# Local and pooled attention ahead of two MoE layers on one core: exponentials of two batches moved to ScalarE, a fixed table of constant products, new urgencies

## The chip, the core and the metric

The kernel runs on one core of a Trainium2 chip. The time is that of the whole program on the device, in microseconds (us); less is better. The engines named below are TensorE (PE; its weight loads PEld), VectorE (DVE), ScalarE (ACT), GpSimd (POOL) and SyncE (SP), which here only issues DMAs.

## The reference

Input q, k, v: 4 batches, 8 heads, 576 positions, 64 columns. Attention is the sum of two parts. The pooled part averages q, k and v over groups of 4 positions (144 left), does a full softmax attention on them and repeats each row 4 times. The local part is softmax attention within 3 positions to either side.

```python
q_d = q.reshape(B, H, Sd, factor, D).mean(axis=3)   # k_d, v_d alike
out_up = np.repeat(sm_attn(q_d, k_d, v_d), factor, axis=2)
scores = np.where(np.abs(i - j) < factor, scale * q @ k.T, -1e9)
out = out_up + softmax(scores) @ v
x = out.transpose(0, 2, 1, 3).reshape(2304, 512)
x = ((x @ w_a) * (x @ w_b)) @ w_out              # first MoE, d_ff 1536
h = x @ w_in
out = (max(h, 0) + alpha * min(h, 0)) @ w_out2   # second MoE, d_ff 2048
```

The four MoE weight matrices come in as float64 (read as int64 words).

## The kernel before

**Plan.** The kernel does not issue instructions directly. Every call goes to a `Plan` (line 22) that records the operation, the regions it reads and writes, and an estimated duration (`cost`, line 94; DMAs in `__call__`, line 128). When all is recorded, `reschedule` (line 214) builds each engine's order by list scheduling: among the ready operations of an engine the one with the highest priority goes first, and a priority is the estimated length of the work behind the operation plus a bias. The bias comes from the call and from the table `URGENT` (line 292) by the name of the operation's group, which `group` (line 1301) derives. Consecutive matmuls inside `with pe()` form one operation; the MoE's groups are chained in a fixed order (`pe(True)`). `fill` (line 257) then looks for planned gaps on TensorE and puts products of a constant bf16 tile (128x128 by 128x256) into them, as many as a share of the gap holds, into a bank that the next group overwrites. `issue` (line 282) sends everything out. Each engine then runs its own list in order and waits on semaphores.

**Attention.** A batch is 6 window tiles of 96 queries and 104 keys, all 8 heads at once. For one tile: `load` (line 670) brings k, q and v by three DMAs; `turn` (678) transposes q and k on TensorE, copies them from PSUM on ScalarE, and VectorE sums groups of four positions for the pooled part; `bound` (693) takes the largest absolute v on VectorE; `soft` (707) adds the mask and the scores into two PSUM banks of four heads, then for each bank VectorE takes the maximum of each row and subtracts it, ScalarE does one exponential over all 832 elements, and VectorE sums, inverts and scales; `p_turn` (731) transposes the probabilities; `av_t` (740) multiplies by v; `x_add` (756) adds the pooled part and splits the sum into two float16 halves in `xt`. The pooled part of a batch: `g_top`, `g_minus`, `g_exp`, `g_out` and `od_turn` for batches 0 and 1; `g_soft`, `g_turn` and `g_av` for 2 and 3. `batch_scale` (786) turns the bounds of a batch into a power of two by `pow2_abs` (440); `pow2_ss` (448) does the same from a sum of squares. Of the eight PSUM banks three ("a") serve attention, four ("m") the MoEs (two of these also the first turns, "h"), one ("r") small maxima.

**MoE.** Matrices are multiplied as three float16 products of high and low halves. `wab_chunk` (993) prepares one of six chunks of w_a and w_b: VectorE narrows float64 words to float32 (three operations of 128x1024 per matrix, `narrow`, line 508), ScalarE squares them for a bound, and ScalarE and VectorE split them (`split`, line 457). `s1` (925) does the first MoE's first products for half a batch: two sums of 12 matmuls of 288 columns, a ScalarE copy out of PSUM, three further operations. `s2`, `s3` and `s4` are the later products; the chain interleaves halves of batches so that attention of the later batches fits beside.

**Order of the recording.** `seq` (from line 1117) lists the head: constants, loads, then turns, softmaxes and the pooled attention of batch 0 interleaved tile by tile, for tiles 0 to 2; tiles 3 to 5, the weight chunks, batches 1 to 3 and the MoEs follow by nominal times.

The lines that the change touches are the DMA estimate (150), `fill`, `URGENT`, `bank` (397), `setup1`, `turn`, `bound`, `soft`, `av_t`, `od_turn`, `x_add`, `batch_scale`, the order of `seq`, `group` and the call of `fill` at the end.

## Time and profile before

| | us |
|---|---|
| median of 3 runs | 1003.62 (1002.61 to 1004.06) |
| the profiled execution, its own time | 1003.87 |
| its span, first to last instruction | 1002.1 |
| TensorE busy | 977.7 (98%) |
| TensorE weight loads busy | 672.5 (67%) |
| VectorE busy | 608.3 (61%) |
| ScalarE busy | 434.4 (43%) |
| GpSimd busy | 39.5 (4%) |

A busy time is the sum over an engine's instructions of that execution, as a share of the span. Constant products count as busy TensorE. All instructions carry line 285, where the plan issues them, so groups are told apart by the tiles that they write and read: `zone` is the large scratch area (attention tiles, later the second MoE's weights), `nm` and `nz` the softmax's maxima and sums, `vst` the bounds on v, `wab` and `wo` the first MoE's weights, `xt` its input, `tm` and `gt` its intermediate tiles, `m`, `a` and `r` the PSUM banks.

### The profile page before, as it was taken

To read this page: it belongs to the slowest core of one execution; us is meant where nothing else is said; L and a number is where in the kernel's file an instruction comes from. 1 tells how busy PE (TensorE), PEld (TensorE's weight loads), DVE (VectorE), ACT (ScalarE), POOL (GpSimd) and SP (SyncE) were. 2 spreads that over 40 slices of the span, in tenths; PEclk is the share of its full clock that TensorE was granted. 3 is DMA by queue.
4 is the path that set the end of the run, shared out by engine and by line. 5 is a ranking of instruction groups with operands and counts; after the bars stand their busy time and mean duration, and the time that the engine had idled before them with its cause. 6 is when DMAs were issued, how large, how long until landed. Compare 5 with 4: busy or idle time off the path is not lost.

```text
span 1002.1 us, 18185 instructions
## 1 busy us (share of the span) xinstructions
PE 977.7 (98%) x7488; PEld 672.5 (67%) x7488; DVE 608.3 (61%) x1293; ACT 434.4 (43%) x919; POOL 39.5 (4%) x81
## 2 busy tenths in 40 slices
PE   6988999999999999999999999999999999999998
PEld 4666777778877788777877777645546455464553
DVE  6899999876657566678987585612406135061340
ACT  3335566544424343335435364623516235162350
POOL 3001300012000200000000000000000000000000
PEclk9999999999999999999999999999999999999999
DMA  9596451144201512323343401010100100200000
GB/s 204 159 270 173 108 153 42 26 75 86 50 1 25 111 26 58 102 67 109 111 159 129 130 1 48 1 43 22 32 32 1 43 22 9 78 2 11 22 1 31
DMA packets 95938, 69.45 MB, mean 69 GB/s; under 512 B 71152, under 2 KB 78704, under 8 KB 95856
## 3 DMA queue, kind: packets, MB, share of 16 engines
q1 hardware_dynamic: 95856, 68.31, 25.2%
q8 instruction: 58, 0.95, 0.4%
q14 instruction: 24, 0.20, 0.1%
HBM read 58.86 MB, written 9.44 MB: 68 GB/s over the span
## 4 chain that ended last, share of the span: by engine, by line
PE 84%; DVE 13%; issue 1%; ACT 1%; DMA 0%; POOL 0%; DVEq 0%; POOLq 0%
PE m L285 75%; PE a L285 8%; DVE wab L285 4%; DVE zone L285 3%; DVE wo L285 2%; DVE nz L285 1%; DVE gt L285 1%; PE r L285 1%; DVE nm L285 1%; DVE tm L285 0%; DVE xt L285 0%; DMA zone<-in_v_dram 0%; DVE vst L285 0%; ACT wo L285 0%; ACT wab L285 0%
## 5 line engine op out<-in xcount | busy, mean ns | idle before, releaser
L285 PEld LDWEIGHTS <-wab 128*128 128x128 f16 x3168 | 306.4, 98 | 161.0 <-issue 4.2
L285 PE MATMUL m<-xt,wab 128*128 128x288 f16 x2304 | 296.2, 286 | 2.5 <-DVE xt L285 2.1
L285 PE MATMUL m<-xt,zone 128*128 128x384 f16 x1152 | 188.2, 326 | 0.0
L285 PE MATMUL m<-zone,wab 128*128 128x512 f16 x864 | 187.7, 379 | 0.0
L285 PEld LDWEIGHTS <-zone 128*128 128x128 f16 x1152 | 112.7, 98 | 74.9
L285 DVE SCALAR_TENSOR_TENSOR gt<-tm,nal,tm 128x384 f32<-128x384 f32 x96 | 59.3, 618 | 160.8 <-ACT tm L285 149.2
L285 PEld LDWEIGHTS <-wo 128*128 128x128 f16 x1152 | 111.8, 98 | 29.5 <-issue 0.8
L285 ACT ACTIVATE tm<-m 128x384 f32<-128x384 f32 (+1 forms) x224 | 95.3, 468 | 65.6 <-PE m L285 65.6
L285 PE MATMUL m<-gt,wo 128*128 128x288 f16 x864 | 110.3, 288 | 0.0
L285 DVE SCALAR_TENSOR_TENSOR wab<-gt,kap,wab 128x384 f16<-128x384 f32 x96 | 59.3, 618 | 58.2 <-ACT wab L285 58.2
L285 ACT ACTIVATE wab<-gt,kap 128x384 f16<-128x384 f32 x96 | 59.0, 615 | 58.1 <-DVE gt L285 58.1
L285 ACT ACTIVATE gt<-m,uf 128x512 f32<-128x512 f32 x18 | 12.4, 687 | 154.2 <-PE m L285 154.2
L285 ACT COPY zone<-a 104x384 f32<-104x384 f32 (+4 forms) x124 | 53.1, 471 | 53.1 <-PE a L285 52.8
L285 PE MATMUL a<-zone 64*96 64x104 f32 (+4 forms) x1104 | 72.8, 265 | 0.6 <-DVE zone L285 0.5
L285 PEld LDWEIGHTS a<-zone 64*96 64x96 f32 (+4 forms) x1104 | 58.4, 149 | 19.9 <-issue 14.6
L285 ACT ACTIVATE zone<-zone 96x832 f32<-96x832 f32 (+3 forms) x49 | 41.9, 855 | 51.8 <-DVE zone L285 49.0
L285 ACT COPY tm<-m 128x288 f32<-128x288 f32 x96 | 37.8, 394 | 43.1 <-PE m L285 40.7
L285 DVE SCALAR_TENSOR_TENSOR tm<-m,tm 128x288 f32<-128x288 f32 x96 | 43.0, 448 | 21.3 <-PE m L285 18.1
L285 ACT ACTIVATE gt<-tm 128x288 f16<-128x288 f32 x72 | 31.6, 440 | 44.4 <-DVE tm L285 44.3
L285 PE MATMUL a<-idf,zone 96*104 96x96 f32 (+4 forms) x392 | 41.6, 247 | 3.8 <-DVE sx L285 1.9
L285 POOL TENSOR_TENSOR zone<-zone 72x256 f32<-72x256 f32 x36 | 31.7, 893 | 307.9 <-DMA zone<-in_v_dram 167.2
L285 DVE SCALAR_TENSOR_TENSOR zone<-zone 128x512 int32<-128x512 int32 (+3 forms) x48 | 40.8, 861 | 0.4
(173 smaller groups left out, 810.5 us busy)
## 6 DMA issues: line engine op xcount, KB each, us to landing
zone<-in_moe_w_in_dram SPq DMA_DIRECT2D x8, 1024.0 KB
zone<-in_moe_w_out_dram SPq DMA_DIRECT2D x16, 512.0 KB
wo<-in_moe_w_a_dram SPq DMA_DIRECT2D x6, 1024.0 KB
wo<-in_moe_w_b_dram SPq DMA_DIRECT2D x6, 1024.0 KB
x_d<-x2s SPq DMA_DIRECT2D x8, 576.0 KB
out_dram<-gt SPq DMA_DIRECT2D x18, 256.0 KB
zone<-in_k_dram SPq DMA_DIRECT2D x21, 208.0 KB
zone<-in_v_dram SPq DMA_DIRECT2D x21, 208.0 KB
```

Of the source, the lines that this page charges most:

```text
L285: f(*args, **kw)
```

## The change

- `soft`: for batches 0 and 1 (`EXPH`) VectorE still takes the maxima, multiplies them by -scale, and ScalarE does one exponential per head (96x104) straight from PSUM, with the maximum as bias and the row's sum as a second output. The two subtractions and the separate sum on VectorE go for these batches.
- `bound`: for batches 0 and 1 (`NORM`) ScalarE squares v and sums it in place of VectorE's maximum; the squares go into the tile's `xt_z` buffer, where nothing reads them. `batch_scale` takes `pow2_ss` for them.
- The tuples `POOLP` and `JOIN` are empty: pooled sums stay on VectorE and `x_add` stays as it is. `setup4` builds a table `up_m` on GpSimd that only the `JOIN` branch reads.
- `fill` takes a table `FILLS`: so many constant products (bf16 tile `warm`, 128x128 by 128x256) go ahead of the named TensorE groups, counted in the order of recording, into the upper half of bank r. There are 187 in 28 places, each issued whatever the plan's gaps are.
- Names that begin with soft, pturn or av of tiles 0 to 2, and the pooled attention of batch 0, take PSUM banks from five (three "a", two "m").
- In the head all six turns come first, then the pooled attention with the softmaxes between, and `p_turn` and `av_t` of tiles 0 to 2 last. Loads are recorded in two calls (k and q; v) with names of their own.
- The planner's estimate of a DMA's rate and issue, the groups' names and the whole table `URGENT` are new.

The diff, with the two tables of urgencies and the branches of empty tuples cut:

```diff
--- before.py
+++ after.py
@@ -147,9 +147,9 @@
             for c in parts:
                 nb *= c
             run = min(min(int(x.ap[-1][1]) for x in (kw["out"], kw["in_"])) * SIZE[el.dtype], 4096)
-            rate = 230e3 if run >= 1024 else 150e3
+            rate = 300e3 if run >= 2048 else 220e3 if run >= 1024 else 195e3
             o.dma = (nb / rate, 2.2)
-            o.dur += 1.0
+            o.dur += 0.8
         else:
             d, o.lag = self.cost(eng, method, out, ins, kw)
             o.dur += d
@@ -254,30 +254,14 @@
         self.order = order
         return order
 
-    def fill(self, t0, t1, chain, early, stat, mov, each):
-
-
...
+    def fill(self, counts, out, stat, mov):
+
+
+        groups = [o for o in self.ops if o.eng == self.PE]
+        for k, n in counts.items():
+            if k < len(groups):
+                o = groups[k]
+                o.calls = [(self.nc.tensor.matmul, (out, stat, mov), dict(start=True, stop=True))] * n + o.calls
 
     def issue(self):
         for o in self.order:
@@ -285,36 +269,47 @@
                 f(*args, **kw)
 
 
-WAY = (0,0,0,0,0)
-
-
-URGENT = {"": -180, "alphas": -80, "bs0": -40, "bs1": 120, "bs2": 35, "bs3": 140, "gexp0": -20, "gexp1": -130,
...
+WAY = (0, 0, 0, 0, 0)
+EXPH, POOLP, NORM, JOIN = (0, 1), (), (0, 1), ()
+NUP = 1
+EARLY = [f"{k}{n}" for k in ("soft", "pturn", "av") for n in range(3)] + ["gtop0", "gminus0", "gexp0", "gout0", "odt0"]
+
+
+FILLS = {0: 22, 2: 3, 9: 4, 11: 4, 17: 1, 18: 1, 19: 3, 20: 2, 28: 5, 29: 5, 30: 4, 31: 11, 35: 1, 37: 2, 38: 6,
+          41: 1, 50: 28, 53: 13, 55: 8, 56: 2, 60: 39, 65: 6, 71: 1, 82: 7, 86: 1, 90: 3, 160: 3, 176: 1}
+
+
+URGENT = {"alphas": -10, "b0@0": 10, "b0@1": 110, "b0@2": 25, "b0@3": -75, "b0@4": -30, "b0@5": 35, "b@1": -80,
...
 
 LAST = None
 
@@ -392,9 +387,12 @@
              "a": [psum.tile([128, 512], F32, name=f"a{i}") for i in range(3)],
              "r": [psum.tile([128, 512], F32, name="r0")]}
     banks["h"] = banks["m"][:2]
+    banks["x"] = banks["a"] + banks["m"][:2]
     nbank = dict.fromkeys(banks, 0)
 
     def bank(tag):
+        if tag == "a" and P.name in EARLY:
+            tag = "x"
         nbank[tag] += 1
         return banks[tag][(nbank[tag] - 1) % len(banks[tag])]
 
@@ -460,6 +458,7 @@
 
     idf = const.tile([128, 128], F32, name="idf")
     ones = const.tile([2, 128], F32, name="ones")
+    warm = const.tile([128, 256], BF16, name="warm")
     floor = const.tile([128, 1], F32, name="floor")
 
     def top_of(m, n):
@@ -608,6 +607,7 @@
     xt_z = [t.rearrange("p (a n) -> p a n", a=KD) for t in
             [const.tile([128, xw], F32, name="xt0")] + [carve(xw) for _ in range(TPB - 1)]]
     odt = carve(KD * NP).rearrange("p (a n) -> p a n", a=KD)
+    up_m = flat(odt)[:HALF, :HALF * FAC]
     vd.append(carve(H * (D + 1))[:HALF].rearrange("p (h d) -> p h d", h=H))
     pt = [raw_z[g][:HALF, :H * NP].rearrange("p (i n) -> p i n", i=H) for g in range(2)]
     od = od_z.rearrange("p (u d) -> p u d", u=2)
@@ -626,6 +626,7 @@
         return (t[:, :H2 * TQ].rearrange("p (a n) -> p a n", a=H2), t[:, H2 * TQ:].rearrange("p (a n) -> p a n", a=H2))
 
     def setup1():
+        V("memset", warm, 1.0)
         for t, n in ((idf, 128), (idb, WK)):
             G("memset", t, 1.0)
             G("affine_select", out=t, in_=t, pattern=[[-1, n]], compare_op=ALU.is_equal, fill=0.0, base=0,
@@ -640,6 +641,13 @@
         G("affine_select", out=pm, in_=pm, pattern=[[4, 3], [FAC, TP]], compare_op=ALU.is_ge, fill=0.0, base=FAC - 1,
           channel_multiplier=-1)
 
+    def setup4():
+        G("memset", up_m, 1.0)
+        G("affine_select", out=up_m, in_=up_m, pattern=[[1, HALF * FAC]], compare_op=ALU.is_ge, fill=0.0, base=0,
+          channel_multiplier=-FAC)
+        G("affine_select", out=up_m, in_=up_m, pattern=[[-1, HALF * FAC]], compare_op=ALU.is_ge, fill=0.0,
+          base=FAC - 1, channel_multiplier=FAC)
+
     def setup2():
         for t in vst:
             V("memset", t, 0.0)
@@ -682,15 +690,29 @@
         qz, kz = qk_of(i)
         t = i % TPB
         for src, n, dst, acc, o in ((rq, TQ, qz, gq_z[b % 2], 0), (rk, WK, kz, gk_z[b % 2], off)):
-            ps = bank(tag)[:, :H2 * n].rearrange("p (a n) -> p a n", a=H2)
+            bk = bank(tag)
+            ps = bk[:, :H2 * n].rearrange("p (a n) -> p a n", a=H2)
+            pq = bk[:, H2 * n:H2 * (n + TP)].rearrange("p (a n) -> p a n", a=H2)
             with pe():
                 for p in range(H2):
                     T("transpose", ps[:, p], src[:, p * 128:(p + 1) * 128], idf[:n, :n])
+                    if b in POOLP:
+                        T("matmul", pq[:, p], src[:, p * 128:(p + 1) * 128], pool_m[:n, o // 4, 48:48 + TP], start=True,
+                          stop=True)
             A("copy", dst, ps)
+            if b in POOLP:
+                A("copy", acc[:, :, t * TP:(t + 1) * TP], pq)
+                continue
             V("tensor_reduce", out=acc[:, :, t * TP:(t + 1) * TP],
               in_=dst[:, :, o:o + TQ].rearrange("p a (n r) -> p a n r", r=FAC), axis=AX.X, op=ALU.add)
 
     def bound(i):
+        b, t = divmod(i, TPB)
+        if b in NORM:
+            r = raw_of(i)[2].rearrange("p h d -> p (h d)")
+            A("activation", out=flat(xt_z[t])[:WK].bitcast(BF16)[:, :H * D], in_=r, func=ACTF.Square,
+              accum_out=vst[b % 2][:WK, t:t + 1])
+            return
         V("tensor_reduce", out=vst[win(i)[0] % 2][:WK, i % TPB:i % TPB + 1], in_=raw_of(i)[2], axis=AX.XY,
           op=ALU.max, apply_absolute_value=True)
 
@@ -717,13 +739,22 @@
             for h in range(H):
                 T("matmul", pss[h % 2][:, h // 2], qz[rows(h), h // 2], kz[rows(h), h // 2], start=False,
                   stop=(h >= H - 2))
+        each = i // TPB in EXPH
         for g in range(2):
             hs = slice(H2 * g, H2 * g + H2)
             V("tensor_reduce", out=m[:, hs], in_=pss[g], axis=AX.X, op=ALU.max)
+            if each:
+                V("tensor_scalar_mul", m[:, hs], m[:, hs], -scale)
+                for h in range(H2):
+                    x = H2 * g + h
+                    A("activation", out=p[:, x], in_=pss[g][:, h], func=ACTF.Exp, scale=scale, bias=m[:, x:x + 1],
+                      accum_out=z[:, x:x + 1])
+                continue
             V("tensor_tensor", out=p[:, hs], in0=pss[g], in1=m[:, hs].unsqueeze(2).to_broadcast([TQ, H2, WK]),
               op=ALU.subtract)
-        A("activation", out=p, in_=p, func=ACTF.Exp, scale=scale)
-        V("tensor_reduce", out=z, in_=p, axis=AX.X, op=ALU.add)
+        if not each:
+            A("activation", out=p, in_=p, func=ACTF.Exp, scale=scale)
+            V("tensor_reduce", out=z, in_=p, axis=AX.X, op=ALU.add)
         V("tensor_scalar_add", z, z, 1e-9)
         V("reciprocal", z, z)
         V("tensor_tensor", out=p, in0=p, in1=z.unsqueeze(2).to_broadcast([TQ, H, WK]), op=ALU.mult)
@@ -740,12 +771,26 @@
     def av_t(i, tag="a"):
 
         ps = bank(tag)[:, :KD * TQ].rearrange("p (a n) -> p a n", a=KD)
...
@@ -790,7 +837,7 @@
         vm = top_of(m, 1)
         sxb[b] = const.tile([128, 1], F32, name=f"sx{b}")
         us = const.tile([128, 1], F32, name=f"ux{b}")
-        pow2_abs(vm, sxb[b], us, up=-1)
+        (pow2_ss if b in NORM else pow2_abs)(vm, sxb[b], us, up=NUP if b in NORM else -1)
         u2b[b] = const.tile([128, 1], F32, name=f"u2{b}")
         V("tensor_tensor", out=u2b[b], in0=us, in1=us, op=ALU.mult)
 
@@ -1120,15 +1167,20 @@
     def add(fn, name="", bias=0.0):
         seq.append((fn, name, bias))
 
+    def add_in(i):
+        add(lambda: load(i, (0, 1)), f"in{i}")
+        add(lambda: load(i, (2,)), f"inv{i}")
+
     add(setup1)
-    add(lambda: load(0))
+    add_in(0)
     add(setup2)
-    add(lambda: load(1))
+    add_in(1)
     add(setup3)
+    add(setup4)
     for i in range(2, TPB):
-        add(lambda i=i: load(i))
+        add_in(i)
     for i in range(3):
-        add(lambda i=i: wab_load(i))
+        add(lambda i=i: wab_load(i), f"wl{i}")
     for i in range(2):
         add(lambda i=i: turn(i, "h"), f"turn{i}")
         add(lambda i=i: v_tile(0, i), f"v{i}")
@@ -1146,30 +1198,29 @@
         add(lambda: v_tile(0, i), f"v{i}")
         add(lambda: bound(i), f"bound{i}")
 
+    turns(2)
+    turns(3)
     tops(0)
-    turns(2)
-    rest(0)
-    turns(3)
+    turns(4)
     tops(1)
-    turns(4)
-    rest(1)
     turns(5)
     for n in range(3):
         add(lambda n=n: g_top(0, n), "gtop0")
     add(lambda: batch_scale(0), "bs0")
     add(lambda: g_minus(0), "gminus0")
-    tops(2)
     for n in range(3):
         add(lambda n=n: g_exp(0, n), "gexp0")
-    rest(2)
+    tops(2)
     for u in range(2):
         add(lambda u=u: g_out(0, u), "gout0")
     add(lambda: od_turn(0), "odt0")
     for i in range(3):
+        rest(i)
+    for i in range(3):
         add(lambda i=i: x_add(i), f"x{i}")
-    head_end = len(seq) * 0.6
+    head_end = len(seq) * 0.4
     for n, (fn, name, bias) in enumerate(seq):
-        on(n * 0.6, fn, name, bias)
+        on(n * 0.4, fn, name, bias)
     T0 = 60.0
     for c in range(DF1 // CW):
         on(8.0 + 10.0 * c, lambda c=c: wab_chunk(c), f"wab{c}", 0.0)
@@ -1301,9 +1352,14 @@
     def group(name):
         kind = name.rstrip("0123456789")
         n = name[len(kind):]
+        if kind in ("in", "inv", "wl"):
+            return name
         if kind in ("turn", "bound", "soft", "pturn", "av", "v", "x", "load") and n:
             b = int(n) // TPB
-            return f"{kind}@{b}" if kind in ("x", "load") else f"t@{b}" if b else f"t0@{n}"
+            if kind in ("x", "load"):
+                return f"{kind}@{b}"
+            k = "p" if kind in ("pturn", "av") else "b" if kind in ("v", "bound") else "t"
+            return f"{k}@{b}" if b else f"{k}0@{n}"
         if name[:3] in ("s1_", "s2_"):
             return f"{name[:2]}@{name[3]}"
         return kind if kind in ("wow", "wos", "wo2w", "wo2s") else name
@@ -1315,8 +1371,7 @@
         P.bias = bias + URGENT.get(P.grp, 0.0)
         fn()
     P.schedule(chain)
-    ib = idf.bitcast(BF16)
-    P.fill(4.0, 200.0, chain, banks["m"][2], ib[:, :128], ib, 0.112)
+    P.fill(FILLS, banks["r"][0][:, 256:], warm[:, :128], warm)
     with tc.manual_schedule():
         P.issue()
```

## Rows read from the trace of the kernel before

**Rows 1.** Table of windows: busy us of each engine, granted TensorE clock, DMA share.
```profile
core 0: us, PE busy (x) PEld busy (x) DVE busy (x) ACT busy (x) POOL busy (x), PEclk, DMA share, GB/s
0.00:34.00 34.00, 25.75 (x190) 17.41 (x190) 21.20 (x45) 11.28 (x21) 7.85 (x45) 0.90 0.93 203
34.00:100.00 66.00, 56.34 (x589) 44.16 (x585) 65.97 (x136) 29.20 (x53) 5.49 (x6) 1.00 0.72 201
100.00:140.00 40.00, 39.42 (x367) 30.96 (x366) 40.00 (x79) 23.34 (x54) 8.14 (x6) 1.00 0.50 139
140.00:180.00 40.00, 38.73 (x359) 30.29 (x360) 40.00 (x99) 27.23 (x57) 0.00 (x0) 1.00 0.18 52
200.00:1002.00 802.00, 797.82 (x5800) 534.83 (x5798) 423.70 (x882) 331.96 (x713) 18.06 (x24) 1.00 0.18 51
```

**Rows 2.** Chain of waits in order of time: start us, us, what.
```profile
164.30 0.95 DVE zone L285
...
166.16 1.47 PE m L285 x12
```

**Rows 3.** Groups by shape, constant products: whole kernel, then 34 to 100 us.
```profile
L285 PE MATMUL m<-idf 128*128 128x256 bf16 x232 | 31.0, 276 | 0.0
...
L285 PE MATMUL m<-idf 128*128 128x256 bf16 x201 | 25.7, 273 | 0.0
```

**Rows 4.** Timeline of TensorE: the first product of the first MoE.
```profile
82.58 0.29 PE L285 MATMUL m<-xt,wab 128*128 128x288 f16 x1
```

**Rows 5.** Groups by shape, whole kernel, VectorE: busy us, mean ns.
```profile
L285 DVE TENSOR_TENSOR zone<-a,nm 96x416 f32<-96x416 f32 x42 | 22.5, 574 | 0.0
...
L285 DVE TENSOR_REDUCE nz<-zone 96x8 f32<-96x832 f32 x21 | 21.2, 1007 | 4.5 <-ACT zone L285 4.5
...
L285 DVE TENSOR_REDUCE vst<-zone 104x1 f32<-104x512 f32 x21 | 14.0, 673 | 0.3 <-DMA zone<-in_v_dram 0.3
...
L285 DVE TENSOR_SCALAR nz<-nz 96x8 f32<-96x8 f32 x24 | 3.8, 158 | 0.1
```

**Rows 6.** Groups by shape, VectorE: 0 to 34, 34 to 100, 100 to 180 us.
```profile
L285 DVE TENSOR_REDUCE nm<-a 96x4 f32<-96x416 f32 x4 | 2.2, 582 | 2.2 <-PE a L285 2.2
...
L285 DVE TENSOR_REDUCE vst<-zone 104x1 f32<-104x512 f32 x3 | 1.9, 672 | 0.0
...
L285 DVE TENSOR_REDUCE vst<-gt 104x1 f32<-104x512 f32 x2 | 1.3, 671 | 0.0
...
L285 DVE TENSOR_REDUCE vst<-x2s 104x1 f32<-104x512 f32 x1 | 0.7, 673 | 0.0
...
L285 DVE TENSOR_REDUCE nm<-a 96x4 f32<-96x416 f32 x10 | 5.4, 575 | 0.0
...
L285 DVE TENSOR_REDUCE nm<-a 96x4 f32<-96x416 f32 x10 | 5.3, 570 | 0.0
...
L285 DVE TENSOR_REDUCE vst<-zone 104x1 f32<-104x512 f32 x4 | 2.7, 668 | 0.0
```

**Rows 7.** Groups by shape, whole kernel, ScalarE: busy us, mean ns.
```profile
L285 ACT COPY tm<-m 128x288 f32<-128x288 f32 x96 | 37.8, 394 | 43.1 <-PE m L285 40.7 <-DVE zone L285 1.1 <-PE a L285 0.8
...
L285 ACT COPY zone<-a 104x384 f32<-104x384 f32 x48 | 20.8, 480 | 24.4 <-PE a L285 24.4
...
L285 ACT ACTIVATE zone<-zone 96x832 f32<-96x832 f32 x21 | 18.8, 897 | 36.2 <-DVE zone L285 36.1
...
L285 ACT ACTIVATE gt<-m,uf 128x512 f32<-128x512 f32 x18 | 12.4, 687 | 154.2 <-PE m L285 154.2
...
L285 ACT ACTIVATE zone<-zone 128x512 bf16<-128x512 f32 x16 | 10.0, 626 | 8.6 <-DVE zone L285 6.0 <-issue 2.6
...
L285 ACT ACTIVATION_READ_ACCUMULATOR zone<-zone 128x1 f32 x24 | 4.5, 189 | 0.0
...
L285 ACT ACTIVATE zone<-a 72x432 f32<-72x432 f32 x8 | 3.8, 519 | 2.7 <-PE a L285 2.7
```

**Rows 8.** Waits of TensorE in the first 100 us: us, times, longest.
```profile
PE m L285 <- POOL one L285: 4.3, 1, 4.3
```

More of the change, by code (lines that the diff above doesn't have):

```diff
@@ L255, in reschedule @@
         return order
-    def fill(self, t0, t1, chain, early, stat, mov, each):
-        pe = [o for o in self.order if o.eng == self.PE]
-        f = self.nc.tensor.matmul
-        add = []
-        for a, b in zip(pe, pe[1:]):
-            n = int((0.3 if a.end < 30.0 else 0.7) * (b.start - a.end) / each)
-            if n < 2 or not t0 <= a.end < t1:
-                continue
-            g = next(o for o in chain if o.start >= b.start)
-            if g is chain[0]:
-                out = early
-            else:
-                if not g.calls[0][2]["start"] or any(p.end > a.end - 0.5 for p in g.preds if p.eng in (self.DVE, self.ACT)
-                                                     and p.name[:2] in ("s1", "s2")):
-                    continue
-                out = g.calls[0][1][0]
-            o = self.new(self.PE)
-            o.calls = [(f, (out[:, :mov.shape[1]], stat, mov), dict(start=True, stop=True))] * n
-            o.start, o.end = a.end + 1e-6, b.start
-            o.name, o.n = "fill", -1
-            add.append(o)
-        self.order = sorted(self.order + add, key=lambda o: o.start)
+    def fill(self, counts, out, stat, mov):
[4 more added lines that the diff above has]
+                o.calls = [(self.nc.tensor.matmul, (out, stat, mov), dict(start=True, stop=True))] * n + o.calls
     def issue(self):
@@ L742, in av_t @@
         ps = bank(tag)[:, :KD * TQ].rearrange("p (a n) -> p a n", a=KD)
+        b, t = divmod(i, TPB)
+        if b in JOIN:
+            u, c = divmod(t, TPB // 2)
+            with pe():
+                for h in range(H):
+                    T("matmul", ps[rows(h), h // 2], raw_of(i)[2][:, h], e_z[i % 2][:, pos(h)], start=(h < 2), stop=False)
+                for h in range(H):
+                    T("matmul", ps[rows(h), h // 2], od[:, u, h * D:(h + 1) * D], up_m[:, c * TQ:(c + 1) * TQ],
+                      start=False, stop=(h >= H - 2))
+            p0 = i * TQ % XR
+            split(ps, sxb[b], xt[:, :KD, p0:p0 + TQ], xt[:, KD:, p0:p0 + TQ])
+            return
         with pe():
@@ L748, in od_turn @@
     def od_turn(b, tag="a"):
+        if b in JOIN:
+            return
         for u in range(2):
@@ L758, in x_add @@
         b, t = divmod(i, TPB)
+        if b in JOIN:
+            return
         p0 = i * TQ % XR
```

56 rows, old and new, of the table URGENT are left out of this document.

## Prediction

> **What bounds the kernel now.** I read the table of windows first, because the page's share of a busy TensorE hides the stages. In it [rows 1] there are three. To 34 us DMA is the load (its engines 93% busy) and VectorE has 12.8 us free. From 34 to 180 us VectorE is busy for 145.97 of 146 us. From 200 us on TensorE is busy for 797.8 of 802 us, and VectorE for half the time. So anything taken from VectorE pays between 34 and 180 us or not at all. The chain of waits agrees [rows 2]: piece after piece of VectorE work up to 164.30 us, then from 166.16 us on TensorE's matmuls to the end.
>
> TensorE's busy time in the VectorE stage is not all useful. The constant products that `fill` puts into gaps are 232 products and 31.0 us of busy time, 201 of them (25.7 us) between 34 and 100 us [rows 3]. In the same 66 us TensorE idles 66.00 - 56.34 = 9.7 us [rows 1], so some 35 us there hold no work of the computation. Between 100 and 166 us hardly anything is lost: idle is 0.6 us to 140 us. The first product of the first MoE stands at 82.58 us [rows 4]. What can be won is that waste of 35 us ahead of 100 us; after 200 us nothing can, since the work there is the same before and after and TensorE does not wait.
>
> **What the change removes from VectorE.** Per window tile of batches 0 and 1 (12 tiles of 24) [rows 5]: two subtractions of 0.574 us, the sum of the exponentials 1.007 us and the bound on v 0.673 us, 2.83 us. Added are two multiplications by -scale on 96x4; the nearest row is a 96x8 one, 0.158 us each, 0.32 us. Net 2.51 us per tile, 30.2 us in all. `pow2_ss` has five operations as `pow2_abs` has: nothing. The pooled sums of q and k stay on VectorE because `POOLP` is empty, and `JOIN` is empty too, so neither branch costs anything.
>
> Not all of it counts. To 34 us VectorE has free time, and there lie all six bounds of batch 0 and two softmaxes [rows 6]. From 34 to 100 us there are 10 half-softmaxes, so 5 tiles; from 100 to 180 us another 5 tiles and 4 bounds, of which one tile and one bound lie past 166 us. A softmax without its bound is 2.51 - 0.67 = 1.84 us. Relief in the binding stage: 5 x 1.84 = 9.2 us to 100 us, and 4 x 1.84 + 3 x 0.67 = 9.4 us from 100 to 166 us.
>
> **What it adds to ScalarE.** One exponential over 832 elements (0.897 us) becomes eight over 104 elements out of PSUM with a bias pointer and a summed output. No row shows that shape. I build it from rows [rows 7]: copies of 384 and 288 elements out of PSUM (0.480, 0.394 us) give 0.9 ns an element, so 0.228 us for 104; the 512-element eviction with a scale pointer (0.687 us) is 0.10 us above the same line drawn from the 432-element exponential (0.519 us), which I take for the pointer; the accumulator's readout is a 0.189 us row. Upper bound 0.52 us each, 4.1 us per tile; lower bound 8 x 0.228 = 1.8 us, if pointer and readout overlap with the neighbours. I take the upper one, since readouts stand as rows of their own. Squares for the bound: 0.626 + 0.189 = 0.82 us [rows 7]. Per tile +3.2 +0.8 = 4.0 us, 48 us over 12 tiles; by the lower bound +1.7 us, 20 us.
>
> Is there cover? ScalarE is busy 79.8 us of the 146 us from 34 to 180 us [rows 1]; 10 softmaxes and 4 bounds bring 35.3 us, to 115.1 us. VectorE falls to 146.0 - 21.1 = 124.9 us. So VectorE is still the fuller engine, by 9.8 us, but each softmax answers later: max 0.577, scaling 0.16, four exponentials twice over, against subtract, 0.897 and sum, about 1 us later per tile, and it holds two of the three `a` banks for that long. I charge nothing for it, since VectorE had no idle time from 34 to 180 us and other work stands ready in its queue while the exponentials run; if that cover goes, it is 1 us for each of the 9 tiles.
>
> **Moves.** In the head all six turns come before the softmaxes, and `p_turn`/`av_t` of tiles 0 to 2 after the global attention: the same instructions, on five banks rather than three. The loads are issued with v apart from q and k: the same 18 issues and bytes on SP, while DMA is the load to 34 us [rows 1]; gain or loss at most the 4.3 us that TensorE waits for its first group [rows 8], I take 0. `setup4` gives POOL a memset and two selections for a table that nothing reads: POOL is busy for 7.9 of the first 34 us and 13.6 of the next 146 us [rows 1], so nothing. One memset of `warm` on VectorE in its free head: nothing. The squares write into the tile buffers `xt_z`, so in batch 1 a bound waits on ScalarE for the same tile's `x_add` of batch 0, done long before; behind it on ScalarE's queue stand the softmax's exponentials, which wait for later events.
>
> **Constant products.** The table holds 187 instead of 232; at 31.0 us / 232 = 0.134 us that is 25.0 us against 31.0 us. They cost nothing where TensorE waits anyhow, and 88 of them stand ahead of four groups (numbers 50, 53, 55, 60: the turns of the probabilities of tiles 3 and 5, the third weight chunk's maximum, tile 4's scores), all of which need a result that VectorE has a part in. I take 0, bounds 0 and +25.0 us. The granted clock is 0.90 of full in the first 34 us and 1.00 in every later stretch [rows 1]; products that kept it up there could win a tenth of 25.75 us, 2.6 us, but that stretch waits for DMA, so I take 0. The new urgencies change the order on every engine; after 200 us TensorE is full in either order, so I charge 0, bounds -4 us (all the idle there, 802.0 - 797.8) and +4 us.
>
> **Sum.** Relief to 100 us in full, 9.2 us, for there TensorE's waste is largest; of the later 9.4 us half, 4.7 us, because TensorE is saturated there and the relief helps only by letting weight preparation come earlier. 13.9 us. The profiled execution took 1003.87 us (span 1002.1 us); its own time stands 0.25 us above the median of 1003.62 us. 1003.87 - 13.9 = 990.0 us.
>
> **The rivals.**
> *The whole relief arrives.* The 18.6 us, and the 7.7 us of the first 34 us as well if the order moves that work behind. Waste of 35 us would allow it; TensorE's full windows after 100 us speak against. 1003.9 - 26.3 = 977.6 us.
> *The table's products land on the path.* They are issued unconditionally and in order. If VectorE's relief makes the four groups ready before TensorE gets to them, 88 x 0.134 = 11.8 us of the gain is given back: 1001.8 us, no change. For it: the old filler sized each group to a planned gap and still left 9.7 us idle; against: the same waits on VectorE exist.
> *ScalarE becomes the bound, slower.* It works in order, so the MoE's copies out of PSUM (0.394 us) stand behind a tile's eight exponentials, and TensorE runs out of its four `m` banks, two pairs of sums at 1.47 us a sum [rows 2], 5.9 us of products. By the sums above it decides once one small exponential costs over 0.52 + 9.8/80 = 0.64 us, or where the waiting for VectorE's maximum adds as much. Fully on the path: 48 - 30 = 18 us, 1022 us; at half, 1013 us. Against: 31 us of ScalarE's 146 stay free. The Trainium skill (Perfetto Trace Analysis, Optimizing Scalar/DVE Operations) says that a saturated engine is better served by fewer, larger operations, which speaks against eight pieces for one; the same section allows moving work to ScalarE when VectorE is saturated, as it is here, and the case hangs on which holds. The skill (ScalarE: Activation LUTs, What ACT_TABLE_LOAD costs) gives 280 ns + 0.833 ns an element for an activation with a bias pointer, by which a piece with its readout would be an estimated 0.56 us and ScalarE would get some 4 us more over 12 tiles than by the rows; the trace of before has no such piece to hold against it.
>
> **How the numbers follow.** Forecast 0.62, whole relief 0.15, products on the path 0.08, ScalarE bound 0.15. About what a measurement of this kernel can tell from no change is 0.2%, 2.0 us. Faster is the first two, 0.77; same 0.08; slower 0.15. The range goes from 976 us (the whole relief and a little of the idle) to 1008 us (half of the way into ScalarE's case), which leaves out a tenth above and less than a tenth below. The forecast's own range is 980 to 1000 us.
>
> **What would show it.** Right: VectorE's busy time 30 us lower over the whole kernel and ScalarE's 48 us higher; small exponentials near 0.32 us with 0.19 us readouts; the first product of the first MoE ahead of 75 us; the chain leaving VectorE before 155 us instead of 166 us; constant products plus idle ahead of 100 us near 30 us instead of 47. Wrong: ScalarE full from 60 to 160 us with TensorE waiting for `m` banks; constant products with no wait after them; or TensorE's idle time after 200 us above 6 us.

## The result, and the profile after

The changed kernel takes 994.62 us (median of 4 runs, 991.76 to 995.89) beside 1003.84 us for the kernel before; the ratio is 0.9916 [0.9898, 0.9934], so by the ratio it is 8.4 us faster. Measured once more beside the second set of experiments it gave 0.9904 [0.9883, 0.9926], 9.6 us; the experiments below are held against 0.991, the middle of the two. The forecast was 990.0 us, 13.9 us faster. The direction was right, and some four to five of the fourteen microseconds did not come.

The page of the changed kernel, its busy times (the instructions now carry line 269):

```profile
PE 972.6 (98%) x7443; PEld 668.4 (67%) x7443; DVE 582.8 (59%) x1270; ACT 461.7 (46%) x1123; POOL 41.1 (4%) x84
...
PE 88%; DVE 8%; DMA 1%; SPq 1%; ACT 1%; issue 1%; ACTq 0%
```

VectorE has 25.5 us less, ScalarE 27.3 us more. The last of these lines is the chain's shares by engine. The table of windows, which answers to [rows 1]:

```profile
0.00:34.00 34.00, 28.68 (x224) 18.89 (x226) 21.43 (x54) 18.31 (x63) 8.83 (x48) 0.95 0.89 205
34.00:100.00 66.00, 55.94 (x556) 44.51 (x553) 62.54 (x129) 41.73 (x139) 12.90 (x12) 0.92 0.73 214
100.00:140.00 40.00, 39.08 (x375) 30.68 (x373) 38.80 (x92) 33.87 (x103) 0.00 (x0) 1.00 0.69 166
140.00:180.00 40.00, 40.00 (x381) 31.82 (x379) 32.59 (x96) 32.87 (x101) 0.00 (x0) 1.00 0.07 15
200.00:994.00 794.00, 788.86 (x5714) 527.08 (x5712) 416.91 (x873) 327.24 (x705) 19.34 (x24) 1.00 0.19 52
```

VectorE is no longer full from 34 to 180 us: it is busy for 133.9 of 146 us. TensorE idles 10.1 us between 34 and 100 us, no less than before, and 0.9 us of 80 from 100 to 180 us. The chain of waits leaves VectorE for good 35 us earlier than in [rows 2], and from 45.51 to 54.15 us it now runs over a transfer:

```profile
45.51 8.64 DMA wo<-in_moe_w_b_dram
...
129.64 1.03 DVE zone L269
...
131.64 1.47 PE m L269 x12
```

The timeline of TensorE, products of the first MoE, answers to [rows 4]. They start at 63.18 us in place of 82.58 us, but only a first part, to 70.1 us; the next stand at 93 us.

```profile
63.18 1.65 PE L269 MATMUL m<-xt,wab 128*128 128x288 f16 x12
...
67.00 3.10 PE L269 MATMUL m<-xt,wab 128*128 128x288 f16 x24
92.98 0.28 PE L269 MATMUL m<-xt,wab 128*128 128x288 f16 x1
94.75 1.51 PE L269 MATMUL m<-xt,wab 128*128 128x288 f16 x11 [1.49 <-DVE xt L269]
```

This next part is the second half of batch 0 (tiles 3 to 5), and what it waits for is VectorE's `xt` of these tiles. In the kernel before, the same wait ends at 99.33 us, so the second part comes 4.6 us earlier and not 19:

```profile
99.33 5.92 PE L285 MATMUL m<-xt,wab 128*128 128x288 f16 x47 [0.85 <-DVE xt L285]
```

**Where the time came from.** From the first of the second products (`gt` by `wo`) on, the kernels take the same: it stands at 193.96 us before and 186.34 us after, and 1002.1 - 193.96 = 808.1 us follow it before, 994.2 - 186.34 = 807.9 us after. So all of the gain lies ahead of it. Two tables of windows up to and from that point, first the kernel before, then the changed kernel:

```profile
0.00:193.96 193.96, 174.20 (x1632) 133.38 (x1633) 180.49 (x398) 98.97 (x200) 21.48 (x57) 0.98 0.56 147
193.96:1002.10 808.14, 803.49 (x5858) 539.09 (x5856) 427.85 (x895) 335.42 (x719) 18.06 (x24) 1.00 0.18 51
```

```profile
0.00:186.34 186.34, 170.04 (x1585) 130.55 (x1585) 161.70 (x386) 130.04 (x409) 21.72 (x60) 0.96 0.59 153
186.34:994.20 807.86, 802.52 (x5861) 537.84 (x5858) 421.08 (x886) 331.67 (x715) 19.34 (x24) 1.00 0.18 51
```

VectorE's busy time there falls by 180.5 - 161.7 = 18.8 us. That this is near the relief of 18.6 us that the prediction counted from 34 to 166 us is chance: all 12 tiles lie ahead of the second products, so the changed shapes have some 28.5 us less there, and other work of VectorE now stands there as well (ten splits of 128x512 instead of five, 3.8 us more, are the largest part). The stretch shrinks by 7.6 us. The other 11.2 us became idle time of VectorE (193.96 - 180.49 = 13.5 us before, 186.34 - 161.70 = 24.6 us after). On TensorE the 7.6 us are 3.5 us less idle (19.8 to 16.3), 2.5 us less of constant products (31.0 to 28.5) and 1.7 us less busy time for the other matmuls.

The profiled execution is the longest of the four; in a second profile of the changed kernel (`after_again`, below) the second products stand at 182.98 us, 11.0 us earlier than before, with the same work of VectorE ahead of them and a granted clock of 0.98 in place of 0.96; 991.1 - 182.98 = 808.1 us follow. The kernel before has only one profile, so the size of the gain is taken from the medians.

```profile
0.00:182.98 182.98, 166.40 (x1584) 128.41 (x1585) 161.64 (x386) 129.82 (x409) 24.02 (x60) 0.98 0.60 155
```

The groups of constant products answer to [rows 3]: the changed kernel to 186.34 us and to 100 us, and the kernel before to 100 us (all 187 take 29.3 us):

```profile
L269 PE MATMUL r<-warm 128*128 128x256 bf16 x183 | 28.5, 305 | 2.5 <-DVE warm L269 1.4 <-DVE ux L269 0.9 <-DVE us_ab L269 0.2
...
L269 PE MATMUL r<-warm 128*128 128x256 bf16 x182 | 28.2, 306 | 2.5 <-DVE warm L269 1.4 <-DVE ux L269 0.9 <-DVE us_ab L269 0.2
...
L285 PE MATMUL m<-idf 128*128 128x256 bf16 x215 | 28.8, 276 | 0.0
```

With the idle time ahead of 100 us (5.3 + 10.1 = 15.4 us) that is 43.6 us without work of the computation. By the same sum the kernel before has 8.2 + 9.7 us of idle time [rows 1] and 28.8 us of products, 46.7 us.

The new ScalarE work: the groups by shape, then eight pieces of a tile in the timeline (start, duration).

```profile
L269 ACT ACTIVATE zone<-a,nm 96x104 f32<-96x104 f32 x72 | 23.7, 345 | 5.7 <-DVE nm L269 3.5 <-DVE ws L269 1.1 <-issue 0.9
...
L269 ACT ACTIVATION_READ_ACCUMULATOR zone<-a,nm 96x1 f32 x72 | 14.8, 206 | 0.0
```

```profile
51.41 0.34 ACT L269 ACTIVATE zone<-a,nm 96x104 f32<-96x104 f32 x1 [3.33 <-DVE nm L269]
51.66 0.19 ACT L269 ACTIVATION_READ_ACCUMULATOR zone<-a,nm 96x1 f32 x1
51.75 0.33 ACT L269 ACTIVATE zone<-a,nm 96x104 f32<-96x104 f32 x1
...
54.00 0.63 ACT L269 ACTIVATE xt<-xt,sx 128x384 f16<-128x384 f32 x1
```

A piece is 0.345 us and its readout 0.206 us, but the pieces start 0.32 to 0.34 us apart: most of the readout runs under its neighbours (`e4_no_readout`, below, shows how much of it does not). Eight take 54.00 - 51.41 = 2.6 us. On VectorE, groups by shape, halved counts and the one new shape answer to [rows 5]:

```profile
L269 DVE TENSOR_TENSOR zone<-a,nm 96x416 f32<-96x416 f32 x24 | 12.9, 577 | 0.0
...
L269 DVE TENSOR_REDUCE nz<-zone 96x8 f32<-96x832 f32 x12 | 12.2, 1015 | 4.5 <-ACT zone L269 4.5
...
L269 DVE TENSOR_REDUCE vst<-zone 104x1 f32<-104x512 f32 x12 | 8.1, 675 | 0.2 <-DMA zone<-in_v_dram 0.2
...
L269 DVE TENSOR_SCALAR nm<-nm 96x4 f32<-96x4 f32 x24 | 4.1, 177 | 0.0
```

### The profile page after: what moved, and what is told of

The parts are those of the page before. It is cut to its first block, busy times and chain, and to the rows that moved or that the text cites. A ratio compares the mean times of both kernels' runs of the same rounds, so it can differ in the third digit from the quotient of the medians.

```text
span 994.2 us, 18276 instructions
## 1 busy us (share of the span) xinstructions
PE 972.6 (98%) x7443; PEld 668.4 (67%) x7443; DVE 582.8 (59%) x1270; ACT 461.7 (46%) x1123; POOL 41.1 (4%) x84
## 3 DMA queue, kind: packets, MB, share of 16 engines
q1 hardware_dynamic: 95856, 68.31, 25.5%
## 4 chain that ended last, share of the span: by engine, by line
PE 88%; DVE 8%; DMA 1%; SPq 1%; ACT 1%; issue 1%; ACTq 0%
PE m L269 77%; PE a L269 9%; DVE wab L269 2%; DVE zone L269 2%; DVE wo L269 1%; PE r L269 1%; SPq L269 1%; DMA wo<-in_moe_w_b_dram 1%; DVE xt L269 1%; DMA gt<-in_v_dram 1%; DVE nm L269 1%; ACT zone L269 0%; DVE tm L269 0%; DVE gt L269 0%; DVE nz L269 0%
## 5 line engine op out<-in xcount | busy, mean ns | idle before, releaser
L269 PE MATMUL a<-zone 64*96 64x104 f32 (+4 forms) x1046 | 70.2, 266 | 0.0
L269 PEld LDWEIGHTS a<-zone 64*96 64x96 f32 (+4 forms) x1046 | 56.5, 149 | 18.8 <-issue 15.5
L269 ACT COPY zone<-a 104x384 f32<-104x384 f32 (+4 forms) x119 | 50.6, 470 | 31.7 <-PE a L269 31.4
L269 ACT ACTIVATE zone<-zone 128x512 bf16<-128x512 f32 (+4 forms) x48 | 39.0, 812 | 46.1 <-DVE zone L269 37.2
L269 DVE SCALAR_TENSOR_TENSOR tm<-m,tm 128x288 f32<-128x288 f32 x96 | 42.7, 447 | 18.7 <-PE m L269 15.9
L269 DVE TENSOR_REDUCE zone<-zone 128x96 f32<-128x384 f32 x48 | 24.9, 545 | 32.6 <-ACT zone L269 32.5
```

What stands on the lines that cost most here:

```text
L269: f(*args, **kw)
```

## The experiments

All were timed against the kernel before on the same chip. "Kept order" means that each engine's list of instructions is that of the changed kernel.

### What VectorE's load is worth: more of it

`e1_pad_b1` adds two needless sums to each softmax of batch 1 after the order is made, `e2_pad_b0` the same to batch 0. VectorE's busy time rises from 582.8 to 593.2 and 593.6 us.

```diff
+            padded.append((i, P.ops[-1], p))
...
+    for i, o, p in padded:
+        if 6 <= i < 12:
+            for c, h in ((0, H), (H, H - 1)):
+                o.calls.append((nc.vector.tensor_reduce, (), dict(out=waste[:, c:c + h], in_=p[:, :h], axis=AX.X, op=ALU.add)))
```

> The kernel after with its order kept on every engine, and in each of batch 1's six tiles two more sums on VectorE behind the scaling of the probabilities (1.0 + 0.9 us, 11.3 us in all; nothing reads them). They give VectorE back what the softmax took from it in batch 1, apart from the bounds. Theory, relief pays only ahead of 100 us, where TensorE has gaps: these lie behind that, so at most one tile's 1.9 us is seen, 994 to 997 us (ratio to before 0.990 to 0.993). Rival, VectorE binds up to 130 us and any microsecond on it counts: all of it arrives, 1003 to 1006 us. My prediction's step (half of the later relief): about 1000 us.

> The same two sums in batch 0's six tiles. Two of these tiles are scaled early, so that 4 to 5 of them stand behind 34 us, 7.5 to 9.4 us of VectorE. Theory, relief ahead of 100 us pays in full: 1001 to 1005 us, the gain is gone. Rival, what limits the stretch up to 100 us is the chain of one tile after another or ScalarE's later answer, not VectorE's load: 995 to 998 us.

Batch 1: 1002.29 us, 0.9998 [0.9985, 1.0012], 8.8 us slower than the changed kernel for 10.4 us of work, nearly all of it. So the theory that VectorE counts only ahead of 100 us fell: the windows of `e1_pad_b1` show TensorE idle for 5.0 + 1.7 = 6.7 us between 100 and 180 us, where the changed kernel has 0.9 us.

```profile
100.00:140.00 40.00, 35.04 (x316) 26.73 (x314) 38.33 (x85) 29.87 (x93) 0.00 (x0) 0.96 0.63 161
140.00:180.00 40.00, 38.27 (x353) 30.10 (x353) 36.42 (x103) 31.50 (x101) 0.00 (x0) 1.00 0.04 6
```

Batch 0: 1010.28 us, 1.0069 [1.0048, 1.0091], 15.9 us slower, more than the 10.8 us added and above both expected ranges. Its executions show what goes with the surplus. The profiled one has a span of 999.5 us at a mean granted clock of 0.989, four others 1008.5 to 1008.8 us at 0.981 to 0.983; the changed kernel's two profiles have 994.2 us at 0.993 and 991.1 us at 0.996. In the profiled execution the loss of clock lies between 34 and 100 us, 0.84 where the changed kernel has 0.92 and 0.95:

```profile
34.00:100.00 66.00, 55.24 (x523) 43.17 (x522) 64.30 (x126) 39.92 (x133) 15.58 (x12) 0.84 0.71 206
```

So the profiled execution pays up to the length of the added work, and the four others some 9 us more, with a lower mean clock. No profile of one of those four exists, so where they lose it is not shown.

### The constant products

`e3_no_fill` has none; `e7_more_fill` has 49 more, 20 of them ahead of group 26, a small maximum.

```diff
-FILLS = {0: 22, 2: 3, 9: 4, 11: 4,
...
+FILLS = {}
```

```diff
-FILLS = {0: 22, 2: 3, 9: 4, 11: 4,
...
+FILLS = {0: 22, 2: 16, 26: 20, 9: 4, 11: 4,
...
-          41: 1, 50: 28, 53: 13, 55: 8, 56: 2,
...
+          41: 1, 50: 28, 53: 13, 55: 8, 56: 18,
...
```

> The kernel after without any of its 187 constant products, order kept. If the products stand only where TensorE waits anyhow and keep up its clock: slower, because the granted clock falls between 50 and 100 us, by 1 to 8 us, 996 to 1003 us. Rival of the prediction, products on the path: faster by 5 to 12 us, 983 to 990 us.

> The kernel after with 49 more constant products at three waits of TensorE that stand ahead of a fall of the granted clock in its profile (13 ahead of the first pooled v, 20 ahead of the second step of batch 0's bound, 16 ahead of tile 4's turn of probabilities), order kept. Rival, the shortfall against the forecast is cold clock: the clock stays at 1.00 from 15 to 85 us and the time falls by 2 to 4 us, 991 to 993 us. Theory, VectorE's load decides: within 1 us of the kernel after, 994 to 996 us.

Without them: 1003.37 us, 1.0018 [0.9997, 1.0038], 10.8 us slower and more than the 1 to 8 us expected, although TensorE has less to do. The windows of `e3_no_fill` have the reason in the column of the granted clock: in each of the three stretches from 34 to 100 us it lies between 0.50 and 0.68, and in the first TensorE is busy for 24.1 of 26 us at the lower of its two levels (1.2 of 2.4 GHz), all with work of the computation.

```profile
34.00:60.00 26.00, 24.10 (x190) 20.19 (x186) 15.22 (x36) 9.78 (x31) 1.06 (x2) 0.50 0.78 200
60.00:80.00 20.00, 12.70 (x96) 9.69 (x97) 19.89 (x43) 15.19 (x51) 7.84 (x5) 0.68 0.65 215
80.00:100.00 20.00, 11.12 (x96) 8.10 (x95) 18.58 (x36) 13.08 (x38) 12.80 (x3) 0.66 0.54 165
```

With 49 more: 997.17 us, 0.9949 [0.9934, 0.9965], 3.9 us slower, at a clock of 0.997, and above both expected ranges: the higher clock brought nothing. TensorE's timeline of `e7_more_fill` shows the 20 products waiting 2.43 us for VectorE's read of the small maximum, because they write the same bank `r`, and then standing in front of the product that waits for that read:

```profile
50.34 3.41 PE L269 MATMUL r<-warm 128*128 128x256 bf16 x20 [2.43 <-DVE tr L269]
53.68 0.58 PE L269 MATMUL r<-tr,ones 1*128 1x1 f32 x2
```

In the changed kernel that product has the same wait to itself and starts at 51.56 us, so the 20 products filled none of the wait and came behind it:

```profile
51.56 0.38 PE L269 MATMUL r<-tr,ones 1*128 1x1 f32 x2 [2.43 <-DVE tr L269]
```

`e10_fill_m2` tests this reading: the same table, but the products ahead of group 60 go to a free bank `m`. They clear partial sums of the first MoE there, so its products are changed in this run.

```diff
-                o.calls = [(self.nc.tensor.matmul, (out, stat, mov), dict(start=True, stop=True))] * n + o.calls
+                o.calls = [(self.nc.tensor.matmul, (out[k >= 60], stat, mov), dict(start=True, stop=True))] * n + o.calls
...
-    P.fill(FILLS, banks["r"][0][:, 256:], warm[:, :128], warm)
+    P.fill(FILLS, (banks["m"][2][:, 256:], banks["r"][0][:, 256:]), warm[:, :128], warm)
```

> The kernel after, order kept, with the 49 more constant products of the earlier run, but those ahead of the sixtieth group written into bank m2, which is free until the first MoE, rather than into bank r. In r they waited for VectorE's read of the small maximum and then delayed the next step of batch 0's bound by 2 us. If the bank was what made them cost: TensorE's clock stays at 1.00 from 34 to 60 us, and the time is 1 to 4 us below the kernel after, ratio to before 0.987 to 0.990. If constant products cost wherever they stand: as the earlier run, 0.994 to 0.996.

The delay goes, the time does not: 997.34 us, 0.9953 [0.9937, 0.9968]. The small product now starts at 49.95 us without a wait, and TensorE then waits 5.07 us for VectorE a few groups later (in the second profile of the changed kernel the small product starts at 48.08 us, so its place alone tells little):

```profile
47.59 2.35 PE L269 MATMUL m<-warm 128*128 128x256 bf16 x20
49.95 0.38 PE L269 MATMUL r<-tr,ones 1*128 1x1 f32 x2
...
58.56 1.49 PE L269 MATMUL a<-idf,zone 96*104 96x96 f32 x8 [5.07 <-DVE zone L269]
```

So the bank explains the wait, but not the 3.9 us. Up to the second products `e7_more_fill` has 173.3 - 166.4 = 6.9 us more busy time of TensorE than `after_again` and only 16.6 - 14.5 = 2.1 us less idle time, so most of the added time did not stand where TensorE had waited. What it delayed stays open.

### The changed kernel once more, ScalarE, and the halves of the change

`after_again` is the changed kernel (its time stands above). `e4_no_readout` leaves the row sums out of the 96 exponentials (the scaling then uses constants in place of the sums) and so takes 96 readouts off ScalarE. `e5_undo` keeps the new tables, head order and products, sets `EXPH` and `NORM` empty and is planned anew. `e6_only_move` is the kernel before with only the exponentials, the bounds and `pow2_ss` of the change; its old filler sizes itself and issues 217 products.

> The kernel after unchanged, on the chip of the three runs below, so that they are compared with it there. 0.990 to 0.995 of the kernel before.

```diff
...
+    mute[0].calls += [(nc.vector.memset, (t, 1.0), {}) for t in rings["nz"][1]]
+    for o in mute[1:]:
+        o.calls = [(f, args, {x: y for x, y in kw.items() if x != "accum_out"}) for f, args, kw in o.calls]
```

> The kernel after, order kept, with the 96 small exponentials not summing their rows (their 0.2 us readouts go, about 19 us of ScalarE; the sums are left out of the computation and stand at a constant). Theory, VectorE's load alone binds: within 1.5 us of the kernel after. Rival, ScalarE's later answer and fuller queue take back part of the relief: 4 to 10 us faster than the kernel after, 985 to 990 us.

`e4_no_readout`: 994.0 us, 0.9905 [0.9884, 0.9927], as the changed kernel. ScalarE's busy time falls by only 8.1 us (461.7 to 453.6). Eight pieces now take 1.98 us where they took 2.6 us, so they stand some 0.23 us apart in place of 0.32 us, and a readout adds some 0.09 us:

```profile
48.92 1.98 ACT L269 ACTIVATE zone<-a,nm 96x104 f32<-96x104 f32 x8 [3.33 <-DVE nm L269]
```

These 8.1 us buy nothing, so ScalarE's load does not bound here.

```diff
-EXPH, POOLP, NORM, JOIN = (0, 1), (), (0, 1), ()
+EXPH, POOLP, NORM, JOIN = (), (), (), ()
```

> The kernel after with the exponentials and bounds of batches 0 and 1 back in their old form, planned anew with the new table of urgencies, head order and constant products. Padding VectorE's list in place cost 8 us in batch 1 and 15 us in batch 0; so if the move is the whole gain and the rest of the change is neutral: 1003 to 1006 us. If the rest of the change costs time that the move has to pay for: 1010 to 1020 us. If the rest alone is the gain: 994 to 997 us.

> The kernel before with nothing but the exponentials and bounds of batches 0 and 1 moved to ScalarE, planned anew with the old urgencies and the old filler. If the move pays by itself: 985 to 997 us. If the gain needs the new order: 1000 to 1008 us.

`e6_only_move`: 996.86 us, 0.9942 [0.9921, 0.9963]. The move by itself brings 5.8 us, and the rest of the change some 3 us on top (0.9942 to 0.991; the intervals touch). `e5_undo`: 1026.78 us, 1.0238 [1.0214, 1.0261], above all three expected ranges. Without the move the new order and tables are 23.9 us slower than the old ones: they fit their own load only, so the two halves do not add. The largest of TensorE's waits in `e5_undo` to 186 us (sum, times, longest) is for VectorE, which from 61.4 to 69.4 us does, among weight preparation, two subtractions, a sum and a bound of the old form (2.75 us):

```profile
PE a L269 <- DVE ws L269: 8.1, 1, 8.1
```

### What VectorE's load is worth: less of it

`e8_less_b0` scales two heads of eight and adds the pooled part to one of four column blocks in batch 0, `e9_less_b1` in batch 1; the rest of both steps is left out. VectorE's busy time falls to 576.7 and 578.7 us.

```diff
...
+    for i, o, kw in short:
+        if 0 <= i < 6:
+            o.calls = [(o.calls[0][0], (), kw)]
```

> The kernel after, order kept, with less VectorE work in batch 0's six tiles: the scaling of the probabilities does two heads of eight and the adding of the pooled part one column block of four (left out of the computation), 0.7 + 0.35 us less per tile, 6.4 us in all. Padding cost more than it added there. If VectorE's load still sets the pace ahead of 100 us: 4 to 7 us faster than the kernel after, ratio to before 0.984 to 0.988. If the loss by padding came from a list with no slack and another chain stands right behind VectorE: at most 2 us faster, 0.989 to 0.992.

> The same cut in batch 1's six tiles, 6.4 us less VectorE work, most of it behind 100 us. If TensorE is full there and VectorE only just keeps up (so that more work costs and less work gains nothing): within 1.5 us of the kernel after, ratio to before 0.989 to 0.993. If a microsecond less counts as much as a microsecond more did (0.73 of it): 4 to 5 us faster, 0.985 to 0.988.

`e8_less_b0`: 991.39 us, 0.9892 [0.9872, 0.9912]; `e9_less_b1`: 992.5 us, 0.9904 [0.9888, 0.992]. By the ratios 1.8 us for 6.1 us in batch 0, and 0.6 us for 4.1 us in batch 1, neither clear of its interval. More VectorE work costs nearly its length or more, less of it pays next to nothing: something else stands right behind VectorE. Part of it is TensorE behind 100 us: in `e8_less_b0` the second part of the first MoE starts at 86.63 us, 3.0 us ahead of the 89.61 us of `after_again`, but the second products stand at 181.89 us, only 1.1 us ahead of its 182.98 us. For the stretch ahead of 100 us VectorE's own waits in `e8_less_b0` name two candidates, a load of the second weight chunk and ScalarE:

```profile
DVE wab L269 <- DMA wo<-in_moe_w_b_dram: 3.0, 1, 3.0
DVE tm L269 <- ACT tm L269: 2.4, 1, 2.4
```

### The load of the second chunk

That load is issued at 45.51 us in the changed kernel and lands 8.64 us later (chain above); six loads of batch 1 were issued just ahead of it, from 40.16 us on. `e11_loads_behind` keeps the order everywhere but on SP, where the six go behind it.

```diff
     P.schedule(chain)
+    late = [o for o in P.order if o.eng == P.SP and o.name in ("load6", "load7")]
+    wb = [o for o in P.order if o.eng == P.SP and P.order.index(o) > P.order.index(late[-1])][0]
+    P.order = [o for o in P.order if o not in late]
+    n = P.order.index(wb) + 1
+    P.order[n:n] = late
```

> The changed kernel with the order kept on every engine except SP's queue: the six loads of batch 1 (k, q and v of tiles 6 and 7), which stand just ahead of the second chunk's w_b load at 40 to 45 us, are put right behind it. Theory A, that this load's landing is what ends the early stage once VectorE has been relieved: it is issued some 4 us earlier, lands at about 47 us or before instead of 52 to 54, VectorE's wait for it (0.4 to 3.0 us in the kernels so far) goes, the tiles 6 and 7 are not missed before 65 us, and the ratio to the kernel before falls to 0.983 to 0.989 (2 to 6 us less than the changed kernel). Theory B, that VectorE's own load and TensorE's remaining work stand so close behind that one transfer more or less does not matter: VectorE's wait goes all the same, but the ratio stays at 0.989 to 0.993. If the moved loads come late for the six products that transpose q and k of batch 1, it is above 0.993.

992.9 us, 0.9904 [0.9881, 0.9926], Theory B. The timeline of SP's queue shows the load issued at 37.60 us, ahead of the six (the first of them at 38.07 us):

```profile
37.60 0.37 SPq L269 DMA_DIRECT2D wo<-in_moe_w_b_dram  x1
```

VectorE's waits from 34 to 100 us come to 0.9 us, none of them for a transfer, and VectorE is again busy for 64.78 of these 66 us:

```profile
DVE us_ab L269 <- PE r L269: 0.6, 1, 0.6
DVE wgr L269 <- ACT x2s L269: 0.3, 1, 0.3
...
34.00:100.00 66.00, 55.64 (x564) 44.83 (x562) 64.78 (x133) 42.91 (x143) 20.83 (x12) 0.95 0.73 210
```

Taking away the load's wait alone, or VectorE's work alone, gives nothing that can be told from the changed kernel. Both at once were not tried, so which limit is the last one between 34 and 100 us stays open.

## Why the prediction was right, and where its sum was not

**The bound and the direction.** VectorE did bind from 34 us on, and relief there paid. `e6_only_move` shows it without the new order (-5.8 us), `e1_pad_b1` and `e2_pad_b0` show the reverse.

**The relief itself** was sized well: 30.2 us were forecast (12 x 2.51 is 30.1), the rows of the changed shapes give 12.8 + 12.0 + 7.9 - 4.1 = 28.6 us (halved groups of subtractions, sums and bounds, less the new multiplications), and VectorE's busy time fell by 25.5 us. How it divides over the stages, 18.6 us from 34 to 166 us, was not measured; the 18.8 us above are of another stretch and of other work too.

**What arrives of it** is the term that was too large. "Relief to 100 us in full, 9.2 us" rested on TensorE's waste of 35 us there: that waste was taken for time that would close when VectorE answers sooner. It hardly closed, 46.7 to 43.6 us instead of "near 30". The first MoE started 19 us earlier, as foreseen (ahead of 75 us), but then stopped at about 70 us until VectorE had `xt` of tiles 3 to 5, and that comes 99.33 - 94.75 = 4.6 us earlier. "Of the later 9.4 us half, 4.7 us" came to 3.0 us. The windows from this point to the second products, first before, then after, and the constant products of the first of them:

```profile
99.28:193.96 94.68, 92.78 (x864) 72.35 (x864) 94.05 (x221) 58.88 (x127) 8.14 (x6) 1.00 0.33 89
...
94.70:186.34 91.64, 90.66 (x852) 71.35 (x851) 83.03 (x217) 72.84 (x222) 0.00 (x0) 1.00 0.36 86
...
L285 PE MATMUL m<-idf 128*128 128x256 bf16 x17 | 2.2, 273 | 0.0
```

Before, TensorE had 94.68 - 92.78 = 1.9 us of idle time and 2.2 us of constant products there, 4.1 us in all, so this term promised more than the stretch had to give. In the changed kernel 1.0 us of idle time is left, and `e9_less_b1` shows no clear gain from further relief of batch 1. In the second profile of the changed kernel the wait for `xt` ends at 91.38 us, so the first part is 8.0 us and the second again 3.0 us. The first term thus differs between executions, with the granted clock to 100 us (0.93 and 0.97); what makes it differ was not tested. In place of 13.9 us the whole change brought 8.4 to 9.6 us, the move alone 5.8 us.

**Moves, urgencies and products** were charged at 0 with bounds of 4 us for the urgencies; the runs put them at some 3 us of gain, in the presence of the move, hardly clear of the intervals. Without it they cost 23.9 us more than the old ones, so "0" was no property of the order but of the order with its load. What the products do was looked for in the wrong sign: bounds 0 and +25, while leaving them all out costs 10.8 us.

**ScalarE** was charged 48 us and got 27.3 us. The rows' durations do add up to such a sum (the pieces 31.7 us, their readouts 19.6 us), but the readouts lie for the most part under their neighbours, so 2.6 us a tile and not 4.1 us. The Trainium skill (ScalarE: Activation LUTs, What ACT_TABLE_LOAD costs) gives 280 ns + 0.833 ns an element for an activation with a bias pointer, an estimated 0.37 us here; the trace comes near it (0.345 us). That a readout adds its whole 0.19 us, as the prediction reckoned, the runs do not bear out: it adds some 0.09 us (`e4_no_readout`).

**The rivals.** The whole relief (977.6 us) did not come. Products on the path: without them the kernel gets 10.8 us slower (`e3_no_fill`), so they do not take the missing microseconds on balance; that some of them cost time beneath what they give the clock is not excluded, since 49 more cost 3.9 us (`e7_more_fill`). ScalarE as the bound: `e4_no_readout` and 0.32 us from piece to piece against the deciding 0.64 us speak against it. The advice of the Trainium skill (Perfetto Trace Analysis, Optimizing Scalar/DVE Operations) to prefer few large operations on a saturated engine did not decide here, since ScalarE keeps idle time in every window (its fullest is 100 to 140 us, 33.9 of 40 us); its other half, to move work to ScalarE when VectorE is full, held.

**What would show it.** VectorE -30: came as -25.5. ScalarE +48: +27.3. Pieces near 0.32 us with 0.19 us readouts: 0.345 and 0.206. The chain leaving VectorE before 155 us: 131 us. Waste near 30 us: 43.6 us, which is the sign that the forecast's size was wrong. Of the signs of a wrong direction none came: after 200 us TensorE idles 794.0 - 788.9 = 5.1 us, under the 6 us named.

## What to carry to other kernels

Relief of a full engine pays only up to the next limit, and a waiting TensorE does not tell how far off that is: before crediting a saving in full, look for what would be waited for next. Stage by stage, TensorE's idle time and filler products are about all that a stage can give (here 4.1 us behind 99 us), and how much of them closes is decided by the last result that TensorE needs there (here `xt` of tiles 3 to 5). A cheap pair of runs, the same engine padded and thinned with the order kept, shows whether a kernel stands on one limit or on several level ones. An order and a table of filler products belong to the load that they were made for, so their gain cannot be added to, or parted from, the change that comes with them.

## What the runs showed of the hardware

Leaving out the constant products costs 10.8 us, and what changes in the windows is the granted clock: with them 0.92 from 34 to 100 us in the changed kernel, without them 0.50, 0.68 and 0.66 in its three parts, and real matmuls that run at the lower level. The mean clock also spreads the executions of one program: 999.5 us at 0.989 and 1008.5 us at 0.981 for `e2_pad_b0`.

VectorE is slower beside GpSimd, and GpSimd beside VectorE. A scaling of 96x832 that lasts 1.01 us elsewhere took 1.54 us while GpSimd summed v, and GpSimd's three additions took 3.36 us there where three others take 2.20 us (VectorE's timeline of the changed kernel, then GpSimd's):

```profile
57.05 1.54 DVE L269 TENSOR_TENSOR zone<-zone,nz 96x832 f32<-96x832 f32 x1
...
85.04 1.01 DVE L269 TENSOR_TENSOR zone<-zone,nz 96x832 f32<-96x832 f32 x1
...
55.88 3.36 POOL L269 TENSOR_TENSOR zone<-zone 72x256 f32<-72x256 f32 x3 [46.42 <-DMA zone<-in_v_dram]
...
75.64 2.20 POOL L269 TENSOR_TENSOR zone<-zone 72x256 f32<-72x256 f32 x3 [6.09 <-DMA zone<-in_v_dram]
```

The Trainium skill (SBUF — State Buffer, SBUF: two separate sides) has the two engines block each other fully while one holds the port pair that they share. The trace fits that, 0.53 us longer on VectorE and 1.16 us on GpSimd, but it does not show the ports, so it cannot tell blocking by turns from a slower pace of both.
